# Moving a clamp and two logarithms further ahead of the sums that read them, in a fused attention and MLP kernel

## The chip, the cores and the metric

The kernel runs on one core of a Trainium2 chip. The metric is the device time of one execution in microseconds; lower is better. Three runs of the kernel before took 468.83, 470.17 and 471.85 us, with a median of 470.17 us.

## The reference

Two blocks follow each other. The first is a gated linear recurrence for 4 batches of 8 heads, over 768 steps, with heads of 48 columns:

```python
f = 1.0 / (1.0 + np.exp(-f_logit))
for t in range(S):
    state = f[:, :, t, :, None] * state + np.einsum('bhd,bhe->bhde', k[:, :, t], v[:, :, t])
    y[:, :, t] = np.einsum('bhd,bhde->bhe', q[:, :, t], state)
```

Its output, with the heads side by side, is `x` of 768 x 384 for each batch. The second block mixes along the sequence through a matrix of rank 32, and then has a channel MLP with 1536 inner columns:

```python
h = xt @ U @ V                       # xt: x with sequence and channels exchanged
u = x + h.transpose(0, 2, 1)
out = u + np.maximum(u @ w_ch1, 0.0) @ w_ch2
```

The inputs of the recurrence are 32-bit floats, and its output too. The weights arrive as 64-bit words and are turned into 32-bit floats on the chip.

## The kernel before, in words

**Units.** The recurrence is done in 16 units (`NU`), each of one pair of heads of one batch; there are `HP` = 4 pairs, so that units 0 to 3 are batch 0 and units 4 to 7 are batch 1. A unit has two sides. Its front (`prepare`, L760) makes the decayed keys and queries; its rear (`attend`, L957) makes scores, states and outputs. Each side is a handful of steps, and `front(n, ...)` and `rear(n, ...)` (L1101 and L1110) hand out those that are asked for by name and haven't been handed out yet.

**Three kinds of front.** Units 6 and later (`TURNED` = 6) take the gates with a sigmoid and a scan. Units 0 to 5 take the logarithm of the gates and sum it with TensorE. For units 4 and 5 the steps are these, with the name that `front` knows them by in brackets:

- `bound` ("gates", L884): VectorE raises f_logit to at least -40 (L886).
- `logs_whole` ("read_back", L888): ScalarE takes Exp (L890) and then Ln with a bias of 1 (L812), in place.
- `sums_kept` ("keep", L893): TensorE multiplies the logarithms with a triangle of ones (`log_sums`, L822), 12 matmul records; f of unit n + 2 is loaded; then ScalarE takes exponentials of the sums (L839 to L844).
- `keys` and `queries`: VectorE transposes and multiplies (L754, L792).

Units with an even number have their f, k and q in the tile `late`, units with an odd number in `other`. So a profile line with `late<-late` at L890 or L812 is unit 4, and one with `other<-other` is unit 5 in the stretch around the change.

**The pieces.** TensorE's, VectorE's and ScalarE's instructions are issued in the order in which the program writes them (`manual_schedule`, L1182 and L1183). Between the steps of the recurrence the program puts pieces of the MLP's products. The stretch that matters is the loop at L1282. `start` is one piece, the turn of the last pair of blocks of `x` (L288); `m.firsts[1:]` are 17 pieces of the first product of batch 0. Each is `ch1` (L294): two accumulation groups in one PSUM tile of the pool `ps_mm` (which has two buffers), and a Relu on ScalarE that drains it into `z` (L335). In the trace such a piece is 12 matmul records on L300. After each piece the loop converts one block of weights (two after pieces 0 and 2), and from piece `EARLY` on it takes the next step from the generator `second`.

**The weights.** A block of weights is loaded by SyncE into a staging tile (`start`, L82; `w_raw` has four buffers, and the first blocks of w1 use free `zw` tiles), and converted in two parts: `halves` on ScalarE (L91, L92) and `join` on VectorE (L98 to L100) and GpSimd (L101). `ahead_by` (L112) makes a call that starts the load of a later block and then converts its own. w1 has 12 blocks of 128 columns, numbered 0 to 11 here; piece `ch1(a, j)` reads blocks 2j and 2j + 1. Blocks 0 to 2 are converted before the loop, 3 and 4 after piece 0, 5 after piece 1, 6 and 7 after piece 2, 8, 9, 10 and 11 after pieces 3, 4, 5 and 6. Then come the blocks of w2.

**The steps after unit 4's front.** `second` (L1281) is a chain: the front of unit 4, then `steps(HP, 2 * HP + 1)` (L1126). `steps` takes one unit after another; for unit n it yields the first front step of unit n + 1 where n + 1 is below `TURNED`, then `joined` groups of rear steps, then the rest of the front of unit n + 1. `joined(a, b, c)` (L1118) leaves out empty groups, yields an empty step for each group but one, and then one step that runs all of them. At n = 4 the rear steps of units 2 and 3 have all been taken already, so one group is left.

SyncE's queue issues all loads in one order. f, k, q and v of unit 4 go out in `held` (L1213), behind the first six blocks of w1. Those of unit 5, and five blocks of weights between them, follow at L1251 to L1255.

Of the kernel before, what the change touches and what calls it, by code (L numbers as in the profile page):

```python
# [564 lines left out]
def factored_path(ctx, tc, q, k, v, f_logit, moe_U, moe_V, moe_w_ch1, moe_w_ch2, out, ok):  # L565
# [11 lines left out]
    HP = H // 2  # L577
# [11 lines left out]
    TURNED = HP + HP // 2  # L589
# [40 lines left out]
    def load(n, *names):  # L630

        b, hp = divmod(n, HP)
        for nm in names:
            if nm == "v":
                v_tiles[n] = three.tile([P, NBL, 2, D], F32, name="v_nat")
            for par in range(2):
                head = src[nm][b, 2 * hp + par]
                if nm in "kq" and n < HP:
                    if par == 0:
                        nc.sync.dma_start(  # L640
                            out=packed(n, nm).rearrange("p (h t) -> p h t", h=2),
                            in_=src[nm][b, 2 * hp : 2 * hp + 2].rearrange("h (p c) d -> p h (c d)", p=P),
                        )
                    continue
                if nm == "v" and par:

                    for s in range(2):
                        nc.sync.dma_start(
                            out=v_tiles[n][(1 - s) * C : (2 - s) * C, :, par, :],
                            in_=head.rearrange("(c s p) d -> s p c d", s=2, p=C)[s],  # L650
                        )
                    continue
                if nm == "v" or n < HP or (nm == "f" and n < TURNED):
                    dst = v_tiles[n] if nm == "v" else nat[n % 2][nm]
                    nc.sync.dma_start(out=dst[:, :, par, 0:D], in_=head.rearrange("(c p) d -> p c d", p=P))
                    continue
                head = head.rearrange("(c i) d -> i c d", i=NB)
                for part in range(2):
                    p0 = par * PAD + part * NB
                    n_ch = min(NB, D - part * NB)  # L660
                    nc.sync.dma_start(  # L661
                        out=raw[n % 2][nm][p0 : p0 + NB, :].rearrange("p (c d) -> p c d", d=NB)[:, :, 0:n_ch],
                        in_=head[:, :, part * NB : part * NB + n_ch],
                    )
# [241 lines left out]
    def mixer(b):  # L906
        return Mixer(tc, b, x_tiles[b], U, V, w1, w2, sums if b else None, ident, blocks, out, two, three, zp, ps_big, ps_mm,
                     b == 0, z_all, room if b >= B - 2 else None, FEWER - (b - B + 2) * NCH // 4)
# [192 lines left out]
    def front(n, *names):  # L1101

        if n >= NU:
            return []
        if n not in ahead:
            names_of = ("gates", "keep", "keys", "read_back", "queries", "gates_end", "unpack_k", "unpack_q")
            ahead[n] = dict(zip(names_of, prepare(n)))
        return [ahead[n].pop(nm) for nm in names if nm in ahead[n]]

    def rear(n, *names):  # L1110

        if not 0 <= n < NU:
            return []
        if n not in here:
            here[n] = dict(zip(("kept", "states", "scan", "scores", "read", "inner", "mask", "spread"), attend(n)))
        return [here[n].pop(nm) for nm in names if nm in here[n]]

    def joined(*groups):  # L1118

        groups = [g for g in groups if g]  # L1120
        for _ in groups[1:]:
            yield lambda: None
        if groups:
            yield lambda: [f() for g in groups for f in g]

    def steps(first, last):  # L1126

        def behind(n):

            return HP + 3 <= n < NU - 1  # L1130

        for n in range(first, last):
            if n + 1 < TURNED:
                yield from front(n + 1, "gates")
            if n < NU:
                yield from joined(rear(n - 2, "inner"), rear(n - 1, "scores"), rear(n, "kept"))
            else:
                for piece in rear(n - 2, "inner") + rear(n - 1, "scores"):
                    yield lambda: None
                    yield piece  # L1140
            if behind(n):
                yield from front(n, "read_back", "queries")
            if n + 1 < NU and n + 1 not in v_tiles:
                load(n + 1, "v")
            yield from front(n + 1, *["read_back"] * (n + 1 < TURNED), "gates", "keep", "keys")
            yield from joined(rear(n - 1, "read"), rear(n, "states", "scan"))
            if not behind(n + 1):
                yield from front(n + 1, "read_back", "queries")
            if n + 1 == last:
                yield from rear(n - 1, "inner")  # L1150
                if n + 2 < NU:
                    load(n + 2, "v")

    def attention(pieces, fill):

        for piece in pieces:
            fill()
            piece()
        fill.rest()
# [9 lines left out]
    def start_mixer(b, after, early=(), late=()):  # L1169

        m = mixer(b)
        n = len(after) // 4
        early, late = ([(0, f) for f in of] for of in (early, late))
        pieces = after[:n] + m.before[:1] + early + after[n : 2 * n] + m.before[1:2] + after[2 * n : 3 * n] + late
        pieces += m.before[2:3] + after[3 * n :] + m.before[3:]
        for _, piece in pieces:
            piece()
        return m
# [4 lines left out]
    with tc.manual_schedule(engines={nc.vector.engine, nc.scalar.engine}):  # L1183
# [65 lines left out]
        m = mixer(0)  # L1249
# [27 lines left out]
        loads = loads[early + 3 :]  # L1277
        start = m.before[5:]

        EARLY = 3  # L1280
        second = chain(front(HP, "gates", "read_back", "keep", "keys", "queries"), steps(HP, 2 * HP + 1))  # L1281
        for i, (_, piece) in enumerate(start + m.firsts[1:]):  # L1282
            piece()
            for f in loads[: 2 if i in (0, 2) else 1]:
                loads.remove(f)
                f()
            if i >= EARLY:
                next(second)()
        for f in loads:
            f()  # L1290
        n = len(m.seconds) // (NBL // 2)
        todo, after = m.seconds[:-n], m.seconds[-n:]

        attention(second, Fill(todo, 10 + 10 * HP - (len(start) + len(m.firsts) - 1 - EARLY)))
        n = 2 * HP + 2
        m = start_mixer(1, after, front(n - 1, "read_back", "queries"), front(n, "gates", "keep"))
        for f in to_sum:
            f()
        pieces, fill = steps(n - 1, 3 * HP + 1), Fill(m.main, 10 * HP - 3)
        for _ in range(4):  # L1300
            fill()
            next(pieces)()
    for b in range(2, B - 1):
        if b > 2:
            pieces, fill = steps(b * HP + 1, (b + 1) * HP + 1), Fill(m.main, 10 * HP)
        after = m.after
        attention(pieces, fill)
        m = start_mixer(b, after)
# [7 lines left out]
    todo = m.first(0) + m.ready(0) + m.halved(0)  # L1316
# [6 lines left out]
    def of(i, kind):  # L1323
        if i >= len(pairs):
            return []
        b, a = pairs[i]
        return getattr(mixers[b], kind)(a)
# [3 lines left out]
    todo = of(0, "sums_of_x") + of(0, "fewer")  # L1331
# [302 lines left out]
@with_exitstack  # L1634
def kernel(
    ctx: ExitStack,
    tc: tile.TileContext,
    q: bass.AP,
    k: bass.AP,
    v: bass.AP,  # L1640
    f_logit: bass.AP,
    moe_U: bass.AP,
    moe_V: bass.AP,
    moe_w_ch1: bass.AP,
    moe_w_ch2: bass.AP,
    out: bass.AP,
):


    nc = tc.nc  # L1650
    args = (q, k, v, f_logit, moe_U, moe_V, moe_w_ch1, moe_w_ch2, out)
    flag = ctx.enter_context(tc.tile_pool(name="flag", bufs=1))
    ok = flag.tile([1, 1], I32, name="ok")
    with ExitStack() as inner:
        factored_path(inner, tc, *args, ok)
    tc.mark_branch_hint_location("general", "LikelyTaken", engines=[nc.vector.engine, nc.sync.engine])
    good = nc.values_load(ok[0:1, 0:1], min_val=0, max_val=1)
    with tc.If(good == 0, label="general"):
        with ExitStack() as inner:
            general_path(inner, tc, *args)  # L1660
# [30 lines left out]
```

## Time and profile before

| | |
|---|---|
| median of 3 runs | 470.17 us |
| lowest, highest | 468.83, 471.85 us |
| profiled execution, its own time | 470.41 us |
| its span | 468.6 us |
| TensorE matmuls, busy | 455.2 us (97%) |
| VectorE, busy | 348.2 us (74%) |
| ScalarE, busy | 170.7 us (36%) |
| GpSimd, busy | 49.3 us (11%) |
| L886 bound, units 4 and 5 | start at 61.87 and 79.90 us, 0.45 us each |
| L890 Exp, units 4 and 5 | start at 62.36 and 82.14 us, 0.68 and 0.67 us |
| L812 Ln, units 4 and 5 | start at 63.07 and 82.84 us, 0.68 us each |
| L822 sums, units 4 and 5 | start at 63.81 and 83.58 us, 1.61 us each |

The span runs from the first to the last instruction of the profiled execution; its own time has 1.8 us more around it. In the profile PE is TensorE's matmuls and PEld its weight loads, DVE is VectorE, ACT ScalarE, POOL GpSimd, and SPq the issuing of transfers by SyncE. A bracket at the end of a timeline's line gives the idle time of the engine just before it and what ended it. Times in timelines are counted from the span's start.

### The profile page before, as it was taken

Reading aid. Unit: us, or ns where it says so; the run is one execution under the profiler, and the core shown is the slowest. Engines: PE = TensorE matmul, PEld = TensorE weight load, DVE = VectorE, ACT = ScalarE, POOL = GpSimd, SP = SyncE. Lnnn points to the kernel's source line nnn. Section 1 sums busy time; section 2 is a strip of 40 time slices with the busy share of each in tenths; the row PEclk is TensorE's granted clock in tenths of the full one; section 3 lists DMA queues with packets and bytes.
Section 4 is the critical chain, followed back from the end, with each engine's and each line's share of the span. In section 5 each row is a group of like instructions: output and inputs, shape, how many; then the busy total and the mean of one; then the engine's idle time right before and its main releaser. Section 6 shows DMA issues by size and latency. Waiting matters only on the chain.

```text
span 468.6 us, 13011 instructions
## 1 busy us (share of the span) xinstructions
PE 455.2 (97%) x5627; PEld 393.5 (84%) x5627; DVE 348.2 (74%) x576; ACT 170.7 (36%) x327; POOL 49.3 (11%) x60
## 2 busy tenths in 40 slices
PE   8999989899999999999999999999999999999997
PEld 5876877786666568899898888989989999999996
DVE  6767758788999687667666568977897896858652
ACT  6775766764332124323231323431221311111200
POOL 2002332354100200101010100120000000000000
PEclk9999999999999999999999999999999999999999
DMA  9937897668778813604543130100000000000001
GB/s 196 203 106 189 197 157 212 178 121 110 108 116 127 132 26 41 89 1 80 71 65 60 27 60 2 29 3 21 19 1 1 35 1 17 18 1 35 1 35 39
DMA packets 154855, 34.35 MB, mean 73 GB/s; under 512 B 143206, under 2 KB 153254, under 8 KB 154790
## 3 DMA queue, kind: packets, MB, share of 16 engines
q1 hardware_dynamic: 153990, 33.29, 36.7%
q8 instruction: 46, 0.75, 0.7%
q10 hardware_dynamic: 800, 0.15, 0.2%
q14 instruction: 19, 0.16, 0.1%
HBM read 28.70 MB, written 4.72 MB: 71 GB/s over the span
## 4 chain that ended last, share of the span: by engine, by line
PE 70%; DVE 15%; ACT 4%; issue 4%; DMA 3%; SPq 2%; POOL 1%; DVEq 0%; ACTq 0%; POOLq 0%
PE pw L389 25%; PE pz L300 14%; PE pp L495 12%; PE po L355 5%; DMA w_raw<-in_moe_w_ch_dram 2%; PE pt L822 2%; PE y L1067 2%; PE sc L975 2%; SPq L661 2%; PE y L1085 1%; PE ds L1026 1%; DVE late L860 1%; DVE added L1051 1%; PE pt L1002 1%; DVE w_y L99 1%
## 5 line engine op out<-in xcount | busy, mean ns | idle before, releaser
L300 PE MATMUL pz<-uT,w 128*128 128x256 f32 x492 | 111.1, 382 | 0.4
L300 PEld LDWEIGHTS pz<-uT,w 128*128 128x128 f32 x492 | 91.9, 190 | 13.5 <-ACT uT L289 0.6
L389 PE MATMUL pw<-zw,w_raw 128*128 128x192 f32 x216 | 38.0, 329 | 0.0
L1055 POOL COPY st<-added 128x576 f32<-128x576 f32 x12 | 18.2, 1513 | 187.6 <-DVE added L1051 187.6
L389 PE MATMUL pw<-w,z_all 128*128 128x192 f32 x216 | 37.3, 327 | 0.0
L389 PEld LDWEIGHTS pw<-w,z_all 128*128 128x128 f32 x216 | 35.3, 190 | 0.5
L389 PEld LDWEIGHTS pw<-zw,w_raw 128*128 128x128 f32 x216 | 35.1, 190 | 0.6 <-DVE w_y L204 0.3
L335 ACT ACTIVATE z_all<-pz 128x512 f32<-128x512 f32 x33 | 19.5, 594 | 41.3 <-PE pz L300 40.9
L101 POOL TENSOR_TENSOR w<-w_y,w_r 128x384 int32<-128x384 int32 x24 | 26.6, 1107 | 44.6 <-DVE w_y L100 34.2
L488 ACT ACTIVATE other<-other 128x512 f32<-128x512 f32 x18 | 11.3, 631 | 40.3 <-DVE other L204 40.3
L355 PE MATMUL po<-w,zw 128*128 128x384 f32 x72 | 25.2, 495 | 0.0
L355 PE MATMUL po<-w,z_all 128*128 128x384 f32 x72 | 24.7, 493 | 0.0
L860 DVE TENSOR_TENSOR_SCAN late<-fz,late 128x768 f32<-128x768 f32 x10 | 17.6, 1755 | 9.4 <-ACT fz L855 9.3
L98 DVE TENSOR_SCALAR w_y<-w_y 128x384 f32<-128x384 f32 (+3 forms) x27 | 11.7, 433 | 15.7 <-ACT w_y L91 15.6
L988 DVE TENSOR_TENSOR A<-sc,causal 128x768 f32<-128x768 f32 x16 | 15.2, 951 | 9.5 <-PE sc L975 9.5
L355 PEld LDWEIGHTS po<-w,zw 128*128 128x128 f32 x72 | 13.2, 190 | 9.6 <-issue 0.8
L355 PEld LDWEIGHTS po<-w,z_all 128*128 128x128 f32 x72 | 13.3, 190 | 8.9 <-DVE o L204 0.6
L488 ACT ACTIVATE z_all<-z_all 128x512 f32<-128x512 f32 x12 | 7.6, 630 | 34.1 <-DVE z_all L204 34.1
L1034 ACT COPY added<-ds 48x576 f32<-48x576 f32 (+2 forms) x29 | 17.9, 620 | 4.9 <-PE ds L1026 4.5
L495 PE MATMUL pp<-v_nat,late 128*128 128x128 f32 x152 | 19.1, 275 | 0.0
L1067 PEld LDWEIGHTS y<-st,qT 48*64 48x64 f32 x704 | 13.6, 137 | 6.5 <-issue 4.5
L878 DVE TENSOR_TENSOR_SCAN late<-fz,other 128x768 f32<-128x768 f32 x10 | 18.5, 1851 | 0.2
(227 smaller groups left out, 871.9 us busy)
## 6 DMA issues: line engine op xcount, KB each, us to landing
w_raw<-in_moe_w_ch_dram SPq DMA_DIRECT2D x18, 384.0 KB, 3.9
out_dram<-o SPq DMA_DIRECT2D x17, 192.0 KB, 1.9
v_nat<-in_v_dram SPq DMA_DIRECT2D x16, 144.0 KB, 2.7
v_nat<-in_v_dram SPq DMA_DIRECT2D x32, 72.0 KB, 3.2
zw<-in_moe_w_ch_dram SPq DMA_DIRECT2D x6, 384.0 KB, 4.8
out_dram<-o SPq DMA_DIRECT2D x14, 96.0 KB, 2.2
w<-in_k_dram SPq DMA_DIRECT2D x4, 288.0 KB, 3.8
w<-in_q_dram SPq DMA_DIRECT2D x4, 288.0 KB, 4.3
```

What stands on the lines that cost most here:

```text
L101: nc.gpsimd.tensor_tensor(dst.bitcast(I32), shaped(y.bitcast(I32)), shaped(r), ALU.add)
L300: nc.tensor.matmul(pm[:, i * 2 * P : (i + 1) * 2 * P], lhsT=w1[:, m, o : o + P], rhs=uT[a][:, m, :], start=(m == 0), stop=(m == NDC - 1))
L335: nc.scalar.activation(z[a, c][:, k : k + 2, :].rearrange("p i t -> p (i t)"), pm, AF.Relu)
L355: nc.tensor.matmul(pm, lhsT=z[a, i // NI][:, i % NI, s * P : (s + 1) * P], rhs=w2[:, i, :], start=(i == 0), stop=(i == NFC - 1))
L389: nc.tensor.matmul(W["pm"][:, n * HM : (n + 1) * HM], lhsT=lhs[:, i, :], rhs=rhs[:, i, :], start=(i == 0), stop=(i == NI - 1))
L488: nc.scalar.activation(dst, dst, AF.Relu, scale=float(SIGNS[n]))
L495: nc.tensor.matmul(pm[:, i, r * P : (r + 1) * P], lhsT=room["w"](wn)[:, r * P : (r + 1) * P], rhs=x_node(a, xn), start=((xn, wn) == of[0]) ...
L860: nc.vector.tensor_tensor_scan(backwards(X, S - 1, S), backwards(f, S, S), backwards(ends, S - 1, S), 0.0, ALU.mult, ALU.add,)
L878: nc.vector.tensor_tensor_scan(Y, f[:, 0:S], starts, 0.0, ALU.mult, ALU.add)
L1034: nc.scalar.copy(added[r, 1:].rearrange("p (e c s) -> p e c s", c=NBL, s=2)[:, e], ds[r, :, 0 : NBL * D].rearrange("p s (c e) -> p e c s", ...
L1055: nc.gpsimd.tensor_copy(st, states.rearrange(by_e, c=NCH))
L1067: nc.tensor.matmul(o(c % 2, par, c // 2), lhsT=T["q"][rows[par], chunk[c]], rhs=T["st"][rows[par], c, :], start=(c <= 2), stop=False, skip ...
```

## The change

For unit 4, `bound` is now run before the loop and `logs` after piece 2. `second` begins with unit 4's sums, and its first step is taken after piece 5 instead of piece 3; since it has two steps fewer, unit 4's sums, keys and queries and all that follows stand behind the same pieces as before. The number of portions of the later fill is the same, too: the two changes in its formula cancel.

In `steps`, the first step of the joined group is taken between the bound and the logarithms of unit n + 1, and the logarithms are no longer handed out together with the sums.

```diff
         for n in range(first, last):
-            if n + 1 < TURNED:
-                yield from front(n + 1, "gates")
             if n < NU:
-                yield from joined(rear(n - 2, "inner"), rear(n - 1, "scores"), rear(n, "kept"))
+                group = joined(rear(n - 2, "inner"), rear(n - 1, "scores"), rear(n, "kept"))
+                if n + 1 < TURNED:
+                    yield from front(n + 1, "gates")
+                    yield next(group)
+                    yield from front(n + 1, "read_back")
+                yield from group
...
-            yield from front(n + 1, *["read_back"] * (n + 1 < TURNED), "gates", "keep", "keys")
+            yield from front(n + 1, "gates", "keep", "keys")
...
-        EARLY = 3
-        second = chain(front(HP, "gates", "read_back", "keep", "keys", "queries"), steps(HP, 2 * HP + 1))
+        EARLY = 5
+        second = chain(front(HP, "keep", "keys", "queries"), steps(HP, 2 * HP + 1))
+        bound, logs = front(HP, "gates", "read_back")
+        bound()
         for i, (_, piece) in enumerate(start + m.firsts[1:]):
             piece()
+            if i == EARLY - 3:
+                logs()
...
-        attention(second, Fill(todo, 10 + 10 * HP - (len(start) + len(m.firsts) - 1 - EARLY)))
+        attention(second, Fill(todo, 10 + 10 * HP - (len(start) + len(m.firsts) + 1 - EARLY)))
```

In the built program three instructions stand elsewhere. On VectorE, L886 of unit 4 stands before the join of block 3 and no longer behind that of block 8. On ScalarE, L890 and L812 of unit 4 stand behind the drain of piece 2 and before the halves of block 6, and no longer behind those of block 9. The orders of TensorE, GpSimd and SyncE are the same, and so is every place of unit 5's instructions.

## The prediction

> **What bounds the kernel now.** I read the page first, then the timelines of each engine from 49 to 84 us, then the chain of waits over the same stretch. The page says that TensorE sets the time:
>
> ```profile
> PE 455.2 (97%) x5627; PEld 393.5 (84%) x5627; DVE 348.2 (74%) x576; ACT 170.7 (36%) x327; POOL 49.3 (11%) x60
> ```
>
> 468.6 - 455.2 leaves 13.4 us in which PE does nothing. The timeline of PE and of its weight loads shows where two of these gaps lie. Columns: start us, us busy, engine, line, what, count, and in brackets the idle time and what ended it.
>
> ```profile
> 49.06 13.22 PE L300 MATMUL pz<-uT,w 128*128 128x256 f32 x60
> 63.81 1.61 PE L822 MATMUL pt<-later,late 128*128 128x130 f32 x12 [1.53 <-ACT late L812]
> 65.25 10.84 PE L300 MATMUL pz<-uT,w 128*128 128x256 f32 x48
> 73.23 2.46 PEld L300 LDWEIGHTS pz<-uT,w 128*128 128x128 f32 x12 [0.45 <-issue]
> 76.02 0.58 PE L1002 MATMUL pt<-ident,kz 64*128 64x64 f32 x12
> 83.58 1.61 PE L822 MATMUL pt<-later,other 128*128 128x130 f32 x12 [1.60 <-ACT other L812]
> ```
>
> The sums of unit 4 (late) waited 1.53 us for their logarithms and those of unit 5 (other) 1.60 us. The third gap is small: a break in the weight loads at 73.23. A piece of products is 12 records, so 13.22 / 5 = 2.64 us, and the four pieces after 65.25 begin at 65.25, 67.89, 70.53 and 73.17. Counting the loop's pieces i from 0 (0 is the turn, 1 the first of the products), these four are 6, 7, 8 and 9. Unit 4's logarithms stand behind piece 4, its sums behind piece 5.
>
> What ScalarE does in the meantime:
>
> ```profile
> 54.54 0.60 ACT L335 ACTIVATE z_all<-pz 128x512 f32<-128x512 f32 x1 [0.55 <-PE pz L300]
> 55.62 0.56 ACT L91 ACTIVATE w_y<-w_raw 128x384 f32<-128x384 f32 x1 [0.48 <-DMA w_raw<-in_moe_w_ch_dram]
> 62.36 0.68 ACT L890 ACTIVATE late<-late 128x576 f32<-128x576 f32 x1 [0.18 <-DVE late L886]
> 63.07 0.68 ACT L812 ACTIVATE late<-late 128x576 f32<-128x576 f32 x1
> 65.36 0.56 ACT L91 ACTIVATE w_y<-w_raw 128x384 f32<-128x384 f32 x1 [1.12 <-DMA w_raw<-in_moe_w_ch_dram]
> 68.04 0.60 ACT L335 ACTIVATE z_all<-pz 128x512 f32<-128x512 f32 x1
> 71.63 0.55 ACT L91 ACTIVATE w_y<-w_raw 128x384 f32<-128x384 f32 x1 [2.99 <-DMA w_raw<-in_moe_w_ch_dram]
> 72.55 0.57 ACT L335 ACTIVATE z_all<-pz 128x512 f32<-128x512 f32 x1
> ```
>
> The reader is to see the last three lines. The drain of piece 6 is at 68.04. The drain of piece 7, whose products ended near 70.5, comes only at 72.55, since w1's block 11 stands before it and sat 2.99 us until its data landed. PSUM's products have two buffers, so piece 9 needs piece 7's: 72.55 + 0.57 = 73.12. That is the break at 73.23. So PE is tied here to a landing, not only to its own work. What sets the landing is SyncE's queue:
>
> ```profile
> 61.94 2.94 SPq L661 DMA_DIRECT2D other<-in_q_dram  x4
> 64.98 0.47 SPq L655 DMA_DIRECT2D v_nat<-in_v_dram  x1
> 65.49 2.03 SPq L648 DMA_DIRECT2D v_nat<-in_v_dram  x2
> 67.63 6.33 SPq L82 DMA_DIRECT2D w_raw<-in_moe_w_ch_dram  x5
> ```
>
> It issues without a break up to 67.63, where block 11 goes out; it lands 3.9 us later. The stretches of the windows view show the DMA engines full, with a share (the last but one number) of 0.97 and 1.01:
>
> ```profile
> 49.00:62.20 13.20, 13.20 (x66) 11.32 (x60) 10.82 (x19) 10.01 (x20) 5.45 (x7) 1.00 0.97 199
> 62.20:65.40 3.20, 1.67 (x14) 1.59 (x14) 2.11 (x4) 1.89 (x4) 1.85 (x2) 1.00 1.01 194
> ```
>
> And the chain that ends in unit 5's sums goes back to the same landing:
>
> ```profile
> 67.63 3.91 DMA w_raw<-in_moe_w_ch_dram
> ...
> 82.84 0.69 ACT other L812
> ...
> 83.58 1.61 PE pt L822 x12
> ```
>
> [...] no table load lies between 46 and 104 us, so that the moved logarithms bring none. [...]
>
> **The change, part by part.** No instruction is added or removed.
>
> *Unit 5.* Its bound and logarithms do not move. The built order of each engine is the same there before and after: for n = 4 the joined list has one group only, so that its first piece is the whole of it, and gates, kept, logarithms, sums follow each other as they did. Worth 0; the 1.60 us stay.
>
> *Unit 4's bound (L886, 0.45 us)* moves on VectorE from behind the join of block 8 to before that of block 3, 18 instructions up. Block 2's join ends near 48.2 and the next starts at 50.45, after 2.23 us of idle time: the bound lies in it at no cost. It waits for the f of unit 4, issued at 38.83; at a landing time of 4 to 7 us, as other loads here show, that is 43 to 46. If the cover went, it would delay block 3's join, and piece 3, by 0.45 us. GpSimd's and SyncE's orders are unchanged.
>
> *Unit 4's logarithms (L890 and L812, 0.68 each)* move from behind block 9 to behind the drain of piece 2, ten instructions up. From 55.14 they take 1.37 us less the overlap, to about 56.5, so block 6 begins at 56.5 and not 55.62: 0.9 us late. Behind it are block 7, the drain of piece 3, block 8, the drain of piece 4, block 9. The later loads waited for GpSimd (0.27, 0.83, 0.46 us), so some 0.4 us of the delay is left from block 8 on. Piece 3's drain goes from 57.81 to about 58.4 and ends at 59.0; piece 5 needs that buffer at 49.06 + 4 x 2.64 = 59.6. Cost on PE: 0. At block 9 the logarithms are gone, which pays it back, and block 10 waits for its landing at 65.3 in any case: the 1.12 us of idle time before it become about 2.5.
>
> *The stall before unit 4's sums* goes. The logarithms are over at 56.5, PE is ready at 62.28: -1.53 us there. The sums begin at about 62.3, piece 6 at 63.8, 7 at 66.4, 8 at 69.05 (its buffer is free at 68.04 + 0.60 = 68.64), and 9 is ready at 71.7.
>
> *What is late next* is piece 7's drain. Block 11's load is issued by SyncE at 67.63 for reasons that PE has no part in, lands at 71.55, and the drain follows at 72.55 as before. Piece 9 begins at 73.2 as before: +1.5 us of new waiting. From there unit 4's keys, its transposes (76.02) and piece 10 have the times they had.
>
> Sum: -1.53 + 1.5 = about 0; I allow -0.1. Were piece 9 let go, there is a second gate: unit 5's logarithms end at 83.52, 11.97 us after block 11's landing, and PE stood before them 1.60 us early already. A gain that reached that point would be added to this wait.
>
> Against the profiled execution's own 470.41 us (468.6 span and 1.8 around it) that is 470.3. The median of the runs shown is 470.17, 0.24 lower, and their spread is 3.0 us; on the median's footing I forecast **470.1**.
>
> **The rivals.** *The gain stays (468.9).* 470.41 - 1.53. For it speaks that the stall is real and that landings vary between executions. Against it: block 11 would have to land some 1.5 us earlier, and to pass unit 5's gate too, 1.6 to 1.8 us earlier. Chance 0.16. *Both stalls go (467.3).* 470.41 - 1.53 - 1.60, if unit 5 moved; the built order says that it does not. Chance 0.02. *Slower (471.8).* The logarithms in front of block 6 delay the loop of ScalarE, VectorE and GpSimd that turns w1's blocks, and the delay isn't paid back: 1.37 us at most, 470.41 + 1.37. It decides once the delay outlasts the idle time before block 10, 1.12 + 1.37 = 2.5 us, and the 2.99 before block 11: with 0.9 us and loads landing as they do, no. Chance 0.07. *That the change makes no difference* is my forecast here: it does what it says to one unit, and the time is taken back 10 us later. Chance 0.73; 0.02 for anything else.
>
> **How the numbers follow.** 470.1 is the likeliest case. The range goes from 468.4, under the case of the gain kept, to 471.5, which takes in most of a loop that is not paid back, with the runs' own scatter in both. A measurement of this kernel can tell about 1% from no change, which is 4.7 us; no case with a mechanism reaches that, so nearly all the chance lies within 1%, and the 0.03 on each side is for what I haven't seen.
>
> **What would show it.** Right: unit 4's sums begin near 62.3 with no wait for late L812, L890 stands near 55.2, and PE has a new gap of about 1.5 us before piece 9 near 73.2, with the drain near 72.55 behind the load at 71.6; the sums of unit 5 still wait about 1.6 us near 83.5. Wrong: no gap near 73, PE's timeline 1.5 us earlier beyond 84, or block 10 or 11 without a wait for its DMA.

## The result, and the profile after

The changed kernel took 469.52 us (median of 16 runs, 467.66 to 471.52), and the kernel before, beside it on the same chip, 469.75 us (468.16 to 472.08). The ratio is 0.9996, with a 95% interval of 0.9978 to 1.0014: no difference.

TensorE's total has hardly moved, 454.2 us against 455.2. The first lines of the page of the changed kernel:

```profile
span 466.7 us, 13011 instructions
...
PE 454.2 (97%) x5627; PEld 393.4 (84%) x5627; DVE 348.0 (75%) x576; ACT 170.0 (36%) x327; POOL 49.3 (11%) x60
```

The timeline of TensorE after, over the same stretch (start us, us busy, engine, line, what, count; in brackets the idle time and what ended it):

```profile
47.91 13.22 PE L300 MATMUL pz<-uT,w 128*128 128x256 f32 x60
60.97 1.50 PE L822 MATMUL pt<-later,late 128*128 128x130 f32 x12
62.30 7.93 PE L300 MATMUL pz<-uT,w 128*128 128x256 f32 x36
71.28 2.83 PE L300 MATMUL pz<-uT,w 128*128 128x256 f32 x12 [1.04 <-ACT z_all L335]
74.04 0.58 PE L1002 MATMUL pt<-ident,kz 64*128 64x64 f32 x12
81.62 1.61 PE L822 MATMUL pt<-later,other 128*128 128x130 f32 x12 [1.62 <-ACT other L812]
```

The wait before unit 4's sums is gone. Three pieces later, before piece 9, there is a wait of 1.04 us for the drain of piece 7, which was 0.45 us of weight loads' idle time before. Unit 5's sums wait 1.62 us, as they did.

ScalarE's timeline after shows why:

```profile
53.89 0.68 ACT L890 ACTIVATE late<-late 128x576 f32<-128x576 f32 x1
54.60 0.68 ACT L812 ACTIVATE late<-late 128x576 f32<-128x576 f32 x1
55.19 0.54 ACT L91 ACTIVATE w_y<-w_raw 128x384 f32<-128x384 f32 x1
...
63.92 0.56 ACT L91 ACTIVATE w_y<-w_raw 128x384 f32<-128x384 f32 x1 [2.15 <-DMA w_raw<-in_moe_w_ch_dram]
...
69.66 0.55 ACT L91 ACTIVATE w_y<-w_raw 128x384 f32<-128x384 f32 x1 [2.55 <-DMA w_raw<-in_moe_w_ch_dram]
...
70.55 0.58 ACT L335 ACTIVATE z_all<-pz 128x512 f32<-128x512 f32 x1
```

The logarithms have left the place before the sums; block 11's halves still stand before piece 7's drain, and they still wait for their data. The chain of waits that ends in unit 5's sums begins at the same landing as it did:

```profile
66.28 3.30 DMA w_raw<-in_moe_w_ch_dram
...
71.51 0.98 DVE kz L754
...
78.16 1.10 POOL w L101
...
80.89 0.69 ACT other L812
...
81.62 1.61 PE pt L822 x12
```

From the landing to unit 5's sums it is 81.62 - (66.28 + 3.30) = 12.04 us after, and 83.58 - (67.63 + 3.91) = 12.04 before. The 1.7 us that PE won at unit 4's sums do not enter this figure: the chain runs from block 11's halves over VectorE (unit 4's keys, L754), GpSimd (L101) and ScalarE, and touches, as the profile has it, neither piece 7's drain nor piece 9. So the one landing holds TensorE at two places, by two separate paths.

The two profiled spans differ by 1.9 us all the same, and most of this can't be the change's. All of it stands at unit 5's sums (83.58 against 81.62; from there to the end it is 385.0 us in both). Of the 1.96 us there, 1.15 were there already when piece 1 began (49.06 against 47.91), and before any moved instruction had run: VectorE's join ahead of the moved bound began at 46.88 and 45.73. The other 0.81 is block 11's landing, which came 22.48 us after piece 1's start before and 21.67 after. Part of these 0.81 us was there before the change could act, too. SyncE's queue, whose order is the same in both kernels, ran ahead by more than piece 1 did when it issued unit 4's q, before any moved instruction had run:

```profile
46.63 3.09 SPq L661 DMA_DIRECT2D late<-in_q_dram  x4
```

in the kernel before, and in the changed one:

```profile
44.98 2.96 SPq L661 DMA_DIRECT2D late<-in_q_dram  x4
```

That is 1.65 us against piece 1's 1.15. The timed runs exclude a gain of 1.15 us or more (the interval ends at 0.9978, 1.0 us), but by themselves not one of 0.8 us.

### The profile page after: what moved, and what is told of

Same layout as the page of the kernel before. It is cut to its first block, busy times and chain, and to the rows that moved or that the text cites. A ratio compares the mean times of both kernels' runs of the same rounds, so it can differ in the third digit from the quotient of the medians.

```text
span 466.7 us, 13011 instructions
## 1 busy us (share of the span) xinstructions
PE 454.2 (97%) x5627; PEld 393.4 (84%) x5627; DVE 348.0 (75%) x576; ACT 170.0 (36%) x327; POOL 49.3 (11%) x60
## 4 chain that ended last, share of the span: by engine, by line
PE 71%; DVE 13%; ACT 4%; issue 4%; DMA 4%; SPq 3%; POOL 1%; DVEq 0%; ACTq 0%; POOLq 0%
PE pw L389 25%; PE pz L300 14%; PE pp L495 12%; PE po L355 6%; SPq L661 2%; PE y L1067 2%; DMA w_raw<-in_moe_w_ch_dram 2%; PE ds L1026 2%; PE sc L975 1%; PE pt L822 1%; PE y L1085 1%; DVE kz L754 1%; DVE kz L792 1%; PE pt L1002 1%; DMA v_nat<-in_v_dram 1%
## 5 line engine op out<-in xcount | busy, mean ns | idle before, releaser
L300 PE MATMUL pz<-uT,w 128*128 128x256 f32 x492 | 111.1, 382 | 1.3 <-ACT z_all L335 1.0
L300 PEld LDWEIGHTS pz<-uT,w 128*128 128x128 f32 x492 | 92.0, 190 | 14.4 <-issue 1.4
L101 POOL TENSOR_TENSOR w<-w_y,w_r 128x384 int32<-128x384 int32 x24 | 26.6, 1108 | 43.8 <-DVE w_y L100 32.4
L98 DVE TENSOR_SCALAR w_y<-w_y 128x384 f32<-128x384 f32 (+3 forms) x27 | 10.4, 386 | 15.5 <-ACT w_y L91 15.4
```

Of the source, the lines that this page charges most:

```text
L101: nc.gpsimd.tensor_tensor(dst.bitcast(I32), shaped(y.bitcast(I32)), shaped(r), ALU.add)
L300: nc.tensor.matmul(pm[:, i * 2 * P : (i + 1) * 2 * P], lhsT=w1[:, m, o : o + P], rhs=uT[a][:, m, :], start=(m == 0), stop=(m == NDC - 1))
```

## The experiments

Two gates stood in the prediction: piece 9, which waits for block 11's landing through piece 7's drain, and unit 5's sums, which wait for their logarithms. My theory was that the change wins some 1.5 us at unit 4's sums and these gates take it back. The main rivals were that the moved logarithms cost ScalarE what they save PE, so that no gain was ever there, and that gains are there and simply add up. So I opened each gate alone, both, and each with the kernel before and with the change, and then shut one further.

A gate is here a place where TensorE is held up by that landing. In all profiled executions here the time from unit 5's sums to the end is between 384.9 and 385.1 us. What a run does is therefore read between the start of piece 1 (the first L300 product) and the start of unit 5's sums. Times in us; "wait" is PE's idle time just before:

| | ratio to before, 95% | piece 1 to unit 4's sums | wait there | wait before piece 9 | wait at unit 5's sums | piece 1 to unit 5's sums |
|---|---|---|---|---|---|---|
| before | 1 | 14.75 | 1.53 | 0.45 (weight loads) | 1.60 | 34.52 |
| after | 0.9996, 0.9978 to 1.0014 | 13.06 | none | 1.04 | 1.62 | 33.71 |
| before, unit 5 early | 0.9964, 0.9951 to 0.9977 | 14.77 | 1.54 | 0.51 | none | 33.21 |
| after, unit 5 early | 0.9976, 0.9959 to 0.9993 | 13.05 | none | 1.20 | none | 32.08 |
| after, block 11 early | 0.9955, 0.9932 to 0.9978 | 13.05 | none | none | 1.56 | 32.37 |
| before, block 11 early | 0.9971, 0.9954 to 0.9989 | 14.77 | 1.55 | none | 0.31 | 32.93 |
| before, both | 0.9964, 0.9944 to 0.9985 | 14.74 | 1.52 | none | none | 32.44 |
| after, both | 0.9931, 0.9914 to 0.9947 | 13.05 | none | none | none | 30.65 |
| after, block 11 late | 1.0097, 1.0064 to 1.0131 | 13.06 | none | 5.42 | 0.27 | 39.22 |

### Unit 5's gate, without and with the change

Unit 5's bound goes behind piece 5 and its logarithms behind piece 6, where ScalarE stood idle ahead of block 11's halves (2.99 us in the kernel before, 2.55 us in the changed one). The empty steps keep what follows at its pieces.

```diff
             piece()
+            if i in (5, 6):
+                front(HP + 1, ("gates", "read_back")[i - 5])[0]()
...
-                yield from front(n + 1, "gates")
+                yield from front(n + 1, "gates") or [lambda: None]
...
+                yield from front(n + 1, "read_back") or [lambda: None]
```

(The last line is, in the changed kernel, the existing step with the empty one added.) On the kernel before:

> The kernel before, with unit 5's bound moved behind piece 5 and its logarithms behind piece 6, where ScalarE stood idle; unit 4 as it was. My theory (two gates in a row: the landing of w1's block 11 at piece 9, then unit 5's logarithms at its sums): unit 4's 1.53 us wait stays, unit 5's 1.60 us wait goes, and since nothing behind it is known to be late, 1.6 us are gained, 469.75 to about 468.1; in the profile the sums of unit 5 start 10.4 us after block 11 has landed, not 12.0. Rival (everything behind block 11 moves with its landing whatever the logarithms do): the wait reappears within 20 us and the gain is 0.

Measured: 469.00 us against 470.47, ratio 0.9964 (0.9951 to 0.9977). TensorE's timeline of this run:

```profile
63.91 1.61 PE L822 MATMUL pt<-later,late 128*128 128x130 f32 x12 [1.54 <-ACT late L812]
...
73.79 2.83 PE L300 MATMUL pz<-uT,w 128*128 128x256 f32 x12 [0.51 <-ACT z_all L335]
...
82.35 1.50 PE L822 MATMUL pt<-later,other 128*128 128x130 f32 x12
```

Unit 5's wait is gone, and 1.7 us with it. The sums began 10.3 us after block 11's landing (72.08 us, an estimate: its halves began at 72.16, and 0.08 after the landing in the kernels before and after), where 10.4 had been expected. The same edit on the changed kernel:

> The changed kernel, with unit 5's bound and logarithms moved in the same way: both units stand ahead, as the change's words have it. My theory: unit 4's 1.53 us are still given back at piece 9, so the time is that of the run with unit 5 alone, about 468.1, and PE waits about 1 to 1.5 us for the drain before piece 9. Rival (unit 5's logarithms alone had swallowed unit 4's gain, and the wait at piece 9 is only where it was parked): both gains are had, about 466.6.

Measured: 468.75 us, ratio 0.9976 (0.9959 to 0.9993). With the second gate open, the change still adds nothing that the timed runs can tell: 0.9976 against 0.9964. Its 1.20 us of waiting stand before piece 9, the first gate. Had the change been worth 1.5 us here, the ratio would have been 0.9932 or so, which is outside the interval.

The profile of this run alone would have misled: between piece 1 and unit 5's sums it is 1.13 us shorter than the run before it (32.08 against 33.21). Block 11 landed some 21.8 us after piece 1 here, and some 22.9 there. In these four profiles the two with the change had the earlier landings, by 0.8 and 1.1 us. Whether that is chance in full, no run shows. The timed runs show no gain from it: with unit 5 early the ratio is 0.0012 higher with the change than without, and the two intervals taken together leave room for a gain of about half a microsecond at most.

### The first gate, with and without the change

SyncE issues block 11's load one place earlier, ahead of unit 5's q and v, so that it has landed when ScalarE comes to it.

```diff
-        weights[early + FIRST + 4][0]()
+        for i in (4, 5):
+            weights[early + FIRST + i][0]()
+        weights[early + FIRST + 5] = (lambda: None, *weights[early + FIRST + 5][1:])
```

> The changed kernel, with the load of w1's block 11 sent right behind block 10's, ahead of unit 5's q and v: it should land some 4 us earlier. My theory: the wait before piece 9 goes, and what is then late is unit 5's logarithms, behind w2's first blocks on ScalarE; those come earlier only as far as w2's first landing lets them, by 1 to 2.5 us, so 467.2 to 468.7. Rival (the landing of block 11 has no part in it): 469.5, and a wait of the same size before piece 9 or 10.

Measured: 467.89 us, ratio 0.9955 (0.9932 to 0.9978). TensorE's timeline, then ScalarE's:

```profile
62.93 1.50 PE L822 MATMUL pt<-later,late 128*128 128x130 f32 x12
64.27 10.52 PE L300 MATMUL pz<-uT,w 128*128 128x256 f32 x48
...
82.25 1.61 PE L822 MATMUL pt<-later,other 128*128 128x130 f32 x12 [1.56 <-ACT other L812]
```

```profile
68.45 0.54 ACT L91 ACTIVATE w_y<-w_raw 128x384 f32<-128x384 f32 x1
...
73.51 0.56 ACT L91 ACTIVATE w_y<-w_raw 128x384 f32<-128x384 f32 x1 [3.26 <-DMA w_raw<-in_moe_w_ch_dram]
```

Block 11's halves no longer wait, and pieces 6 to 9 run as one stretch of 48 records. But the next load, w2's first block, now has the wait (3.26 us until 73.51), and unit 5's logarithms, which stand behind it, are 1.56 us late as before. So the change's gain passed the first gate here and stopped at the second.

If that is so, the same edit without the change should be worth as much, the 1.5 us being waited for at unit 5's sums if they aren't at unit 4's:

> The kernel before with w1's block 11 sent right behind block 10. With block 11 early and unit 5 as it was, the changed kernel took 0.9955 of the kernel before, and PE still waited 1.56 us at unit 5's sums. My theory: here unit 4's 1.53 us wait stays, PE reaches unit 5's sums 1.5 us later, just when their logarithms are ready, so the wait there is under 0.3 us and the time is the same as with the change: 0.9955, about 468. The change is worth nothing here either, because of the second gate. Rival (only the landing of block 11 hid the change's gain, so that it shows once block 11 is early): 1.5 us slower than the changed kernel with block 11 early, 0.9987.

Measured: 468.38 us, ratio 0.9971 (0.9954 to 0.9989), between the theory's and the rival's numbers. The interval takes in the theory's 0.9955, and just reaches the rival's 0.9987. TensorE's timeline speaks for the theory, not quite in full:

```profile
63.56 1.61 PE L822 MATMUL pt<-later,late 128*128 128x130 f32 x12 [1.55 <-ACT late L812]
65.00 10.52 PE L300 MATMUL pz<-uT,w 128*128 128x256 f32 x48
...
81.72 1.61 PE L822 MATMUL pt<-later,other 128*128 128x130 f32 x12 [0.31 <-ACT other L812]
```

Unit 4's sums wait 1.55 us and unit 5's only 0.31: most of what PE lost at the one it didn't wait for at the other. Of the 1.7 us that the change takes from unit 4's wait, 32.93 - 32.37 = 0.56 were left at unit 5's sums. 0.30 of these is w2's first block, whose halves began 23.63 us after piece 1 with the change and 23.93 without. The other 0.26 is unit 4's wait itself, come through by another way. From those halves to unit 5's sums it is 82.25 - 73.51 = 8.74 us with the change, and 81.72 - 72.72 = 9.00 without, since ScalarE stood still once more, for PE's own products of piece 10:

```profile
78.86 0.60 ACT L335 ACTIVATE zw<-pz 128x512 f32<-128x512 f32 x1 [0.54 <-PE pz L300]
79.36 0.58 ACT L91 ACTIVATE w_y<-w_raw 128x384 f32<-128x384 f32 x1
80.29 0.67 ACT L890 ACTIVATE other<-other 128x576 f32<-128x576 f32 x1
80.99 0.68 ACT L812 ACTIVATE other<-other 128x576 f32<-128x576 f32 x1
```

By these two timelines the waiting of this run goes back from unit 5's sums through this drain and pieces 10 to 6 to unit 4's sums and their logarithms, and not to w2's landing. With block 11 early, then, the theory is right but for some 0.3 us: that much of the change's gain is no longer taken back.

### Both gates open

Both edits together, on the changed kernel:

> The changed kernel with both: unit 5 ahead and block 11 sent earlier. My theory: both gates are open, so unit 4's 1.53, unit 5's 1.60 and the 0.24 at piece 9 of the kernel before are all had: 469.75 - 3.4 = about 466.4, and PE has no wait over 0.5 us from piece 1 to the sums of unit 5. Rival (the next load, w2's first blocks, takes block 11's place as the gate): no better than either alone, 467.5 to 468.2, with a wait for a drain before piece 10 or 11.

and on the kernel before:

> The kernel before with both gates opened: block 11 early and unit 5 ahead, but unit 4 as it was. The same two edits on the changed kernel gave 0.9931. My theory: now nothing hides unit 4's wait, so this kernel is 1.5 us slower than that one: 0.9931 + 0.0033 = 0.9964, and PE waits 1.5 us at unit 4's sums and nowhere else up to unit 5's sums. Rival (the change has no worth of its own): 0.9931, with the wait made up later.

Measured: 466.93 us, ratio 0.9931 (0.9914 to 0.9947), with the change; 467.62 us, ratio 0.9964 (0.9944 to 0.9985), without. TensorE's timeline with the change has no wait from piece 1 to unit 5's sums:

```profile
62.79 1.50 PE L822 MATMUL pt<-later,late 128*128 128x130 f32 x12
64.13 10.52 PE L300 MATMUL pz<-uT,w 128*128 128x256 f32 x48
...
75.11 5.45 PE L300 MATMUL pz<-uT,w 128*128 128x256 f32 x24
80.39 1.50 PE L822 MATMUL pt<-later,other 128*128 128x130 f32 x12
```

Without the change one wait is left, unit 4's:

```profile
64.58 1.61 PE L822 MATMUL pt<-later,late 128*128 128x130 f32 x12 [1.52 <-ACT late L812]
66.02 10.52 PE L300 MATMUL pz<-uT,w 128*128 128x256 f32 x48
...
82.28 1.50 PE L822 MATMUL pt<-later,other 128*128 128x130 f32 x12
```

From piece 1 to unit 5's sums that is 30.65 against 32.44 us: here the change is worth 1.79 us. The timed ratios differ by 0.0033, 1.6 us, but the intervals touch, and the two ran on different chips. So I ran both kernels again, on one chip:

> The changed kernel with unit 5 ahead and block 11 early once more, beside the same without the change on one chip, since 0.9931 and 0.9964 came from two chips' runs. My theory: 0.993 again, 3.2 us less than the kernel before, and 1.5 us less than its neighbour without the change. Rival (the 1.5 us between the two was the difference of the chips): the same as its neighbour within 0.5 us.

> The kernel before with unit 5 ahead and block 11 early, unit 4 as it was, on the same chip as its neighbour with the change. My theory: 0.9964 again, 1.7 us less than the kernel before, because unit 4's wait of 1.5 us is in the open. Rival: 0.993 as its neighbour.

Measured: 466.27 us, ratio 0.9933 (0.9897 to 0.9969), with the change; 467.57 us, ratio 0.9959 (0.9943 to 0.9974), without. The difference is 0.0026, 1.2 us. These intervals overlap too, so that the size of the gain rests on the profiles, and its sign on two pairs that agree. Four of the eight runs with the change are below 466.54 us, the lowest of the 22 without. The profile of the first of the two repeats 30.65 us to the hundredth. The second's profiled execution had a mean clock of 0.989 and slow stretches before piece 1 (the four records of L318 at 46.56 us took 2.08 us, against 1.13 us in the first's), and I don't rest anything on its 32.06 us (it would make the change worth 1.41).

The rival by which the logarithms cost ScalarE what they save PE is out: with the gates open, the same move is worth what was waited for before it. The kernel with the change and both edits is also the fastest here, 0.69% under the kernel before.

### The first gate shut further

Last, block 11's load is issued three places later, behind the next three blocks'. If the landing sets what follows, the time must grow by what the landing moves.

```diff
         written.close()
+        turns_of = [w[0] for w in weights[early + 11 : early + 15]]
+        for i, f in enumerate(turns_of[1:] + turns_of[:1]):
+            weights[early + 11 + i] = (f, *weights[early + 11 + i][1:])
```

> The changed kernel with w1's block 11 sent behind the first three blocks of w2 and not before them: it should land about 3.3 us later. My theory: the wait before piece 9 grows from 1 to about 4 us, unit 5's sums start 12 us after the landing as before, and the time rises by nearly as much, 2.5 to 3.3 us, to about 472.4. Rival (PE has slack of its own behind piece 9): no more than 1 us slower.

Measured: 474.59 us, ratio 1.0097 (1.0064 to 1.0131), 4.6 us more than before; I had expected 2.5 to 3.3. TensorE's timeline and ScalarE's:

```profile
61.86 1.50 PE L822 MATMUL pt<-later,late 128*128 128x130 f32 x12
...
76.55 5.30 PE L300 MATMUL pz<-uT,w 128*128 128x256 f32 x12 [5.42 <-ACT z_all L335]
...
88.02 1.61 PE L822 MATMUL pt<-later,other 128*128 128x130 f32 x12 [0.27 <-ACT other L812]
```

```profile
74.93 0.54 ACT L91 ACTIVATE w_y<-w_raw 128x384 f32<-128x384 f32 x1 [6.77 <-DMA w_raw<-in_moe_w_ch_dram]
```

The direction and the place are as expected: one load was moved behind three others in SyncE's queue, and PE stands before piece 9 for 5.42 us. The size was off for two reasons. The data landed at 74.85, 26.05 us after piece 1 and not 21.67, which is 4.4 us later where I had put 3.3. Only 1.5 us of these are the later issue (19.86 us after piece 1 against 18.37); the other 2.9 lie between issue and landing, 6.19 us against 3.30:

```profile
68.66 6.19 DMA w_raw<-in_moe_w_ch_dram
```

And piece 9 then took 5.30 us instead of 2.83. The windows of this run show the second one (the columns are the stretch and its length, the busy time of PE, PEld, DVE, ACT and POOL, then PE's granted clock, the DMA share and GB/s):

```profile
70.00:76.50 6.50, 1.13 (x6) 0.65 (x4) 0.92 (x3) 1.57 (x4) 0.00 (x0) 0.86 0.70 193
76.50:82.00 5.50, 5.45 (x18) 4.09 (x20) 5.36 (x9) 2.39 (x6) 1.99 (x2) 0.54 0.41 108
82.00:88.00 6.00, 5.75 (x36) 4.71 (x32) 5.23 (x11) 5.41 (x11) 2.09 (x2) 1.00 0.75 200
```

The clock granted to TensorE is 0.54 from 76.50 to 82.00, while piece 9 runs. From the landing to unit 5's sums it was 88.02 - 74.85 = 13.17 us, 1.1 more than the 12.04 of the kernels before and after; the chain of waits now goes through piece 9. 4.4 + 1.1 = 5.5 is what the profile has between piece 1 and unit 5's sums, 39.22 against 33.71 of the changed kernel. Against the 34.52 of the kernel before it is 4.7, close to the 4.6 of the timed runs.

## Why the prediction was right, point by point

*What bounds the kernel.* Right. Piece 9 and unit 5's sums hang on one landing, shown by moving it: later, and the time grows by 4.6 us; earlier, and it falls, by 0.45% with the change and 0.29% without. (With unit 5 opened as well it falls by 0.69%, but of this unit 5's own edit is a part.)

*Unit 5: 0.* Right: 1.62 us of waiting against 1.60.

*Unit 4's bound at no cost.* Right. It ran at 46.99, straight behind the join before it and inside the idle time of VectorE, whose next join began at 49.31.

*The logarithms delay block 6 by 0.9 us, and PE pays nothing.* Right. L890 began 5.98 us after piece 1 (6.1 in the prediction's numbers), block 6 began 7.28 us after piece 1 against 6.56 before, 0.72 late, and the five pieces up to unit 4's sums ran without a gap. The idle time before block 10 went from 1.12 to 2.15 us; I had put 2.5.

*The stall at unit 4's sums: -1.53.* Right in kind, a little small: piece 1 to unit 4's sums fell from 14.75 to 13.06. The term should have been -1.7. The difference of 0.16 is an overlap: without a wait the sums began at 60.97, before the recorded end of the products ahead of them (47.91 + 13.22 = 61.13), where with the wait they began 1.53 us behind that end (63.81 against 49.06 + 13.22 = 62.28). Another 0.11 was won behind the start of the sums, whose group took 1.61 us after the wait and 1.50 without one.

*What is late next: +1.5 before piece 9.* Right in place and cause, too large. Piece 9 begins 2.76 us ahead of the transposes (74.04 - 71.28), so before it began at 73.26. From the start of unit 4's sums to it were 9.45 us before and 10.31 after: 0.86 us of new waiting. 1.7 won less 0.86 leaves the 0.8 by which the landing came earlier after piece 1 in this execution, and piece 9 with it. I had taken the landing as fixed, and it isn't to better than a microsecond (21.67 to 22.94 us after piece 1 in four profiles). No run ties the 0.81 us to the change, and some 0.5 of them stood in SyncE's queue before any moved instruction had run.

*The sum, about 0.* Right, and for the reason given. Against the profiled execution's 470.41 us the new one has 468.38, but 1.15 of these 2.0 us lie before piece 1, and of the other 0.8 some 0.5 stood in SyncE's queue before the change could act; the timed ratio is 0.9996. That it is so close to 1 is in part luck: its interval is about 0.8 us wide on each side.

*The rival "the gain stays".* Its condition was not enough. I had written that block 11 would have to land 1.6 to 1.8 us earlier to pass unit 5's gate too. With block 11 alone early enough not to be waited for at all, unit 5's sums still waited 1.56 us, since the next block of weights took over as the late landing. The prediction's chain stopped at the first late load; the second stood right behind it in SyncE's queue. And the edit that let the gain through, opening both gates, needed unit 5's logarithms moved, not an earlier landing alone.

*The rival "both stalls go", 467.3.* The number fits what opening unit 5 as well as piece 9 gives (466.9), but it takes more than moving unit 5: with unit 5 alone moved, the changed kernel took 468.75.

## What to carry to other kernels

Before a step is moved out of an engine's way, follow that engine to its next wait: if that one ends at a transfer that the engine has no part in, what is won is waited away there, as 0.86 of the 1.7 us won at unit 4's sums were before piece 9. Where several waits follow each other and the later ones end at late transfers, they have to be opened together, and an early one can look worthless, as unit 4's did here (0.9996 alone, 1.2 to 1.8 us with the others open). Look at what stands ahead of the instruction that frees a buffer, in its engine's order: here a conversion on ScalarE that waited 2.99 us for its data held up piece 7's drain in the kernel before until 72.55 us, 2 us after the products had ended (near 70.5).

## What the hardware showed beside this

One long wait cost more than its length. In the run with block 11 late TensorE stood still for 5.42 us (71.13 to 76.55). The clock granted to it was 1.00 from 40 to 70 us, 0.87 from 74 to 75, 0.50 from 75 to 81, 0.72 from 81 to 82, and 1.00 from 82 to 120. Taken as steps between 1.00 and 0.50, these means put the drop at 74.74, 3.6 us after the last product, and the return at 81.56, 5.0 us after the next one began (an estimate from the 0.87 and the 0.72). The 12 records of piece 9, nearly all within that time, took 5.30 us, against 2.83 in the changed kernel. All six runs of this kernel had a mean clock of 0.989 to 0.996; of the 34 runs of the kernel before beside them, 27 had 0.999 or more. Shorter waits came without such a drop: in the changed kernel the clock was 1.00 from 60 to 72 us, around the wait of 1.04, and the profiled executions of the kernel before (1.53 and 1.60 us) and of the five runs that waited 1.20 to 1.56 us at one place had means of 1.000. How long a wait has to be for it, one run doesn't show.

Two more profiles had a lower mean clock: 0.996 in the changed kernel with both edits, and 0.989 in the repeated kernel without the change; the repeated kernel with the change had 1.000. If all of it was at half, that is 3.7 us of the first's span of 465.3 us and 10.3 of the second's 469.8 (an estimate from these means). In both it lies ahead of piece 1. The first has the same 30.65 us from piece 1 to unit 5's sums as the repeat at 1.000, and the same 384.9 us from there to the end. In the second, the groups of four L318 records from 46.56 and 48.97 us took 2.08 and 1.79 us, and the one from 51.21 us 1.13; piece 1, at 52.79, and the four pieces behind it took 13.22 us, as everywhere. So no figure of the table above is touched; what caused the two is open.
